# A Fourier-mixing and expert kernel: step A's start, four of its groups, and the order of its first loads are changed

## The chip, the cores and the metric

The kernel runs on one core of a Trainium2 chip. The metric is the device time of one execution in microseconds (us), the median of several runs. Lower is better.

## The reference

The input x is 4 sequences of 3008 rows with 256 channels, float32. Each sequence goes through a real Fourier transform along its rows; the spectrum is multiplied by a complex 256 x 256 matrix, gets a bias, is shrunk towards zero by 0.01 (real and imaginary parts apart) and is transformed back. The 12032 rows then pass a feed-forward block whose weights arrive as 64-bit floats:

```python
X = np.fft.rfft(x, axis=1)
Yr = Xr @ w_r - Xi @ w_i + b_r
Yi = Xr @ w_i + Xi @ w_r + b_i
Yr = np.sign(Yr) * np.maximum(np.abs(Yr) - lam, 0.0)      # Yi alike
y = np.fft.irfft(Y, n=x.shape[1], axis=1)
h = x @ w_in                                              # 256 -> 2048
g = np.maximum(h, 0.0) + alpha * np.minimum(h, 0.0)
return (g @ w_out).astype(np.float32)                     # 2048 -> 256
```

## The kernel before

A transform of length 3008 = 47 x 64 is done in two steps of matrix products. **Step A** (`a_mm`, `a_evac`) multiplies the rows by a table of 94 x 96; a sequence has 16 groups of 512 columns. **Step B** (`b_load`, `b_mm`, `b_evac`, `b_evac2`) is the second half, in 12 blocks q, each on data that a DMA has reordered. **M** (`m_mm`, `m_evac`) mixes channels and shrinks. **C** (`c_mm`, `c_evac`) and **D** (`d_load`, `d_mm`, `d_part`) transform back; between them the data goes through DRAM (`zd`). Then come the two layers of the expert block, `l1_step` and `l2_step` for the first part of the rows and a form with fewer products (`s_l1`, `s_l2`) for the rest. The Fourier stages of sequences 1 to 3 are laid between the expert steps of the sequence before. Sequence 0 has nothing to hide behind, and the change lies there.

A product of float32 operands takes two passes of TensorE here. The other way is to split an operand into a high and a low fp32r part (`split`: ScalarE copies the high part, another engine subtracts it to get the low one) and to make three fp32r products. Step A of sequences 0 and 1 uses float32 and the table `lf_s`; sequences 2 and 3 use `a_split` and the split table `la_s` (L392 to L394). The mixing weights `wr_s`, `wi_s` are split once, in `split_mix`, from tiles that `load_mix` fetches.

The order of work is written out by hand; each engine executes its own instructions in that order. At the start SyncE (SP) issues the loads: eight pairs of groups of x, four slices of the table rb, four groups of sequence 1, the mixing weights, more of rb, two blocks of raw expert weights (`conv_load`). GpSimd (POOL) issues small tables and the bias. TensorE executes products of a zeroed tile `idle` (`keep_warm`) that nothing reads: 36 ahead of step A, 70 ahead of step B, 12 ahead of step D. Step A runs through the 16 groups of sequence 0 and 4 of sequence 1, with three PSUM buffers (tag "f"); even groups are evacuated by ScalarE (ACT), odd ones by VectorE (DVE), those of sequence 1 by ScalarE. After group 15, POOL issues six DMAs (L420) that bring blocks q = 0 to 2 of the evacuated `a0_s` into `bt`, which has three buffers; `split_mix` and `bias_parts` follow. The tiles of two of the later ScalarE evacuations (tags "Yt", "Yc") are those that `bias_parts` reads from.

Then a loop over t = 0 to 12 does `b_mm(t)`, `m_mm(t-1)`, `c_mm(t-3)` on TensorE and, on the other engines, evacuations and `pump(n)`: n portions of the conversion of raw 64-bit expert weights into two fp32r parts, on ScalarE, VectorE and GpSimd. The list `PT` says how many portions belong to each t. In the same loop stand the later loads: `b_load(t+3)`, rb, cf, and rows of sequence 1 (`a_load(1, g)`), among them one group of eight DMAs (g = 6). SP and ScalarE issue DMAs into eight completion semaphores in turn; a DMA waits for the one that had its semaphore before. After the loop, `TAIL` finishes M and C, loads D's first input (`d_load`) and fills the wait with ten groups of step A of sequence 1 (`a_fill`).

Of the kernel before, what the change touches and what calls it, by code (L numbers as in the profile page):

```python
# [93 lines left out]
def fft_mix_moe(ctx, tc, x, w_r, w_i, b_r, b_i, w_in, w_out, alpha, la, rb, lc, rd, lf, cf, sel, out):  # L94
    nc = tc.nc
# [35 lines left out]
    V, G, A, PE = nc.vector, nc.gpsimd, nc.scalar, nc.tensor  # L131

    def f(t):
        return t.bitcast(F32)

    def split(src, hi, lo, e_hi, e_lo):

        if e_hi is A:
            A.activation(out=hi, in_=src, func=AF.Copy)
        else:  # L140
            e_hi.tensor_copy(out=hi, in_=src)
        e_lo.tensor_tensor(out=lo, in0=src, in1=f(hi), op=ALU.subtract)


    la_s = const.tile([NP, 2, NQ], F32R, name="la_s")
# [37 lines left out]
    def first_bias():  # L183

        raw = work.tile([4, 2, C], F32, tag="Yt", name="bias_f", bufs=1)
        hi = work.tile([4, 2, C], F32R, tag="Yc", name="bias_h", bufs=1)
        pick = work.tile([4, 129], F32, tag="ot", name="sel", bufs=1)
        nc.gpsimd.dma_start(out=pick, in_=sel)
        for i, b in enumerate((b_r, b_i)):
            for k in range(2):  # L190
                nc.gpsimd.dma_start(out=raw[2 * i:2 * i + 2, k], in_=b.unsqueeze(0).to_broadcast([2, C]))
        rows = const.tile([128, 2, C], F32R, tag="bias", name="bias_p")
        ones = const.tile([128, 128], F32R, tag="wd", name="ones")
        V.memset(f(rows), 0.0)
        V.memset(f(ones), 0.0)
        bias[0] = ones, rows

        def parts():
            V.memset(lam_s, -LAM)
            V.tensor_copy(out=ones[0:4], in_=pick[:, 0:128])  # L200
            V.tensor_copy(out=hi, in_=raw)
            V.scalar_tensor_tensor(out=rows[0:4], in0=f(hi), scalar=pick[:, 128:129], in1=raw, op0=ALU.mult, op1=ALU.add)

        return parts
# [20 lines left out]

    def split_mix():
        for t, w in zip(mix_w, mix):
            split(t, w[:, 0], w[:, 1], A, G)
        mix_w.clear()

    def combine_mix():
# [22 lines left out]
    def conv_load():  # L254

        m, i = divmod(conv_m[0], 2)
        conv_m[0] += 1
        k = conv_m[0] % 3
        raw = cw_s[:, NSLOT + 8 * k:NSLOT + 8 * k + 8].rearrange("p (k n) f -> p k (n f)", k=2)
        raw = raw.rearrange("p k (n w) -> p k n w", w=2)  # L260
        src = w_out.bitcast(U32)[256 * m:256 * m + 256] if i else w_in.bitcast(U32)[:, 512 * m:512 * m + 512]
        nc.sync.dma_start(out=raw.rearrange("p k n w -> p k (n w)"), in_=src.rearrange("(k p) f -> p k f", p=128))
        conv_raw.append((raw, m, i))
# [70 lines left out]
    def put(*queues):  # L334
        for n, (o, i) in enumerate(stores):
            (queues or (nc.sync,))[n % max(len(queues), 1)].dma_start(out=o, in_=i)
        stores.clear()
# [3 lines left out]
    def a_load(b, g):  # L341

        if g == 0:
            ad[b] = dram.tile([NQ, R, C], F32, tag="ad", name=f"ad{b}")
        src = x[b].rearrange("(p r) c -> p r c", r=R)[:, 4 * g:4 * g + 4]
        if b == 0:
            ts = [x_s[:, 4 * g:4 * g + 4]]
        elif b == 1 and g in X1_TAGS:
            tags = X1_TAGS[g]
            ts = [work.tile([NP, 4 // len(tags), C], F32, tag=tag, name="xt", bufs={"Yl": None, "gh": 4}.get(tag, 1))  # L350
                  for tag in tags]
        else:
            ts = [work.tile([NP, 4, C], F32, tag="xt", name="xt")]
        if (b, g) == (0, 0):
            ts = [ts[0][:, 0:2], ts[0][:, 2:4]]
        n = 4 // len(ts)
        for i, t in enumerate(ts):

            for p in ((0, 80), (80, NP)):
                nc.sync.dma_start(out=t[slice(*p)], in_=src[slice(*p), n * i:n * i + n])  # L360
        xt[b, g] = ts
# [8 lines left out]
    xp = {}  # L370

    def a_split(b, g):

        t, = x_rows(b, g)
        hi = work.tile([NP, 2, C], F32R, tag="xh", name="xh")
        lo = work.tile([NP, 2, C], F32R, tag="xl", name="xl")
        split(t, hi, lo, A, V)
        xp[b, g] = hi, lo
# [3 lines left out]
    def a_mm(b, g):  # L382
        ps = ps_f.tile([NQ, 2, C], F32, tag="f", name="ps_a")
        pa[b, g] = ps
        if b < 2:
            ts = x_rows(b, g)
            n = 2 // len(ts)
            for i, t in enumerate(ts):
                PE.matmul(ps[:, n * i:n * i + n], lf_s, t, start=True, stop=True)
            return  # L390
        hi, lo = xp.pop((b, g))
        PE.matmul(ps, la_s[:, 0], hi, start=True, stop=False)  # L392
        PE.matmul(ps, la_s[:, 1], hi, start=False, stop=False)
        PE.matmul(ps, la_s[:, 0], lo, start=False, stop=True)  # L394

    def a_evac(b, g):
        ps = pa.pop((b, g))
        if b == 0:
            st = a0_s[:, g]
        else:  # L400
            tag = A1_TAGS[g] if b == 1 and g < len(A1_TAGS) else "zst"
            st = work.tile([NQ, 2, C], F32, tag=tag, name="ast", bufs={"bt": 3, "zst": 3, "Yt": 1, "Yc": 1}.get(tag))
        if b == 0 and g % 2:
            V.tensor_copy(out=st, in_=ps)
        else:
            A.activation(out=st, in_=ps, func=AF.Copy)
        if b:
            stores.append((ad[b][:, 2 * g:2 * g + 2], st))
# [562 lines left out]
    PAT = [0, 0] + [1] * 46  # L971
    NG = R // 2
    EARLY = 4
    FILL = 14
    C0 = 2
    PT = [1, 2, 3, 3, 3, 3, 3, 3, 3, 3, 4, 4]
    TAIL = [['me', 1], ['ce', 3], ['cm', 2], ['cm', 1], ['ce', 2], ['ce', 1], ['d'], ['f', 4], ['e'], ['f', 6]]
    WARM = 70
    A1_TAGS = ("zst", "zst", "Yt", "Yc", "bt", "bt", "bt", "Xh", "Xl", "Xh", "Xl", "zst", "zst", "Yc")
    X1_TAGS = {4: ("Yl", "Yl"), 5: ("os", "Yt"), 6: ("gh",) * 4}  # L980
    idle = const.tile([128, 128], BF16, name="idle")

    def keep_warm(n):
        ps = ps_f.tile([128, 512], F32, tag="f", name="ps_idle")
        for _ in range(n):
            PE.matmul(ps[:, 0:128], idle, idle, start=True, stop=True)

    with tc.manual_schedule():
        nc.gpsimd.dma_start(out=lf_s, in_=lf)
        bias_parts = first_bias()  # L990
        nc.gpsimd.dma_start(out=la_s, in_=la)
        V.memset(idle, 0.0)
        keep_warm(36)
        for g in range(NG // 2):
            a_load(0, g)
        load_rb(0, 4)
        for g in range(EARLY // 2):
            a_load(1, g)
        load_mix("Yh", "Yh")
        load_rb(4, 12)  # L1000
        conv_tags.update(v1=("yh", "yl"), ex=("xh", "xh"), lf=("xl", "xl"))
        for _ in range(C0):
            conv_load()
        seq = [(0, g) for g in range(NG)] + [(1, g) for g in range(EARLY)]

        for n, (b, g) in enumerate(seq):
            a_mm(b, g)
            if n >= 1:
                a_evac(*seq[n - 1])
            if n == NG:  # L1010
                for q in range(3):
                    b_load(0, q)
                split_mix()
                bias_parts()
        a_evac(*seq[-1])
        half(0)
        put()
        load_tables()
        keep_warm(WARM)

# [3 lines left out]

        a1 = [EARLY]
        hold = []

        def a_fill(n):
            for g in range(a1[0], min(a1[0] + n, FILL)):
                a_mm(1, g)  # L1030
                a_evac(1, g)
                a1[0] = g + 1

        for t in range(NPAIR + 1):
            run(b_mm, t)
            run(b_load, t + 3)
            run(c_evac, t - 4)
            run(b_evac, t)
            run(m_evac, t - 2)
            run(m_mm, t - 1, ps_h)  # L1040
            run(b_evac2, t)
            run(c_mm, t - 3)
            if t < NPAIR:
                pump(PT[min(t, len(PT) - 1)])
            if t in (2, 5):
                load_rb(2 * t + 8, 2 * t + 14)
            if t < 8 and t % 2 == 0:
                load_cf(3 * t, 3 * t + 6)
            if 5 <= t < 10:
                a_load(1, t - 3)  # L1050
            if t == 10:
                half(1)
                conv_m[1] = FT
# [17 lines left out]
                {"me": m_evac, "cm": c_mm, "ce": c_evac}[op](0, NPAIR - args[0])  # L1071
        V.tensor_scalar(out=beta_s, in0=alpha_s, scalar1=-1.0, scalar2=1.0, op0=ALU.mult, op1=ALU.add)
        conv_tags.update(v1=("xh", "xl"), ex=("Yh", "Yh"), lf=("Yl", "bt"))
        keep_warm(12)
        for c in range(2):
            d_open(c)
            d_step(0, c)
# [22 lines left out]
        for b in range(B):  # L1100
# [9 lines left out]
            if b == 0:  # L1110
                for g in range(FILL, NG):
                    i = 6 * (g - FILL) + 9
                    if g % 2 == 0:
# [84 lines left out]
        for k in range(len(spairs) + SLAG):  # L1198
# [9 lines left out]
            if k >= SLAG:  # L1208
                n, t = spairs[k - SLAG]
# [43 lines left out]
```

## Time and profile before

| | |
|---|---|
| median of 3 runs | 1350.11 us (1349.89 to 1350.86) |
| the profiled execution's own time | 1351.47 us |
| its span in the profile | 1349.7 us |
| TensorE (PE) busy | 1334.4 us, 99% of the span |
| TensorE weight loads (PEld) | 1250.5 us, 93% |
| VectorE (DVE) | 1035.8 us, 77% |
| ScalarE (ACT) | 760.9 us, 56% |
| GpSimd (POOL) | 379.0 us, 28% |

Busy time is the time in which an engine has an instruction at work; matmuls are pipelined, so a busy TensorE is not one at its peak. The span goes from the first to the last instruction; about 1.8 us of the execution lie outside it. The times of rows count from the span's start. A releaser (after "<-") is what ended an engine's idle time, as inferred from semaphores. "SPq" and "ACTq" are DMA issues on the queues of those engines.

### The profile page before, as it was taken

The page shows a single profiled execution, that of the slowest core. Times are in us where ns is not written, and L with a number is a line of the kernel's source. Part 1 is how long each engine was busy: PE and PEld are TensorE (multiplying, and loading weights), DVE is VectorE, ACT ScalarE, POOL GpSimd, SP SyncE. Part 2 cuts the span into 40 slices and gives each one's busy share as a digit, 9 for nine tenths or more (in the row PEclk, how much of TensorE's full clock was granted, in tenths as well). Part 3 has the DMA queues.
Part 4 walks back from the last instruction along what each step waited for, and adds up shares of the span by engine and source line. Part 5 has one row for each costly group of instructions (what it writes and reads, how often), then busy time and mean ns, then how long its engine had stood idle before and what let it go on. Part 6 is the DMA issues. An engine that isn't in the chain of part 4 may idle for free.

```text
span 1349.7 us, 25116 instructions
## 1 busy us (share of the span) xinstructions
PE 1334.4 (99%) x9200; PEld 1250.5 (93%) x9200; DVE 1035.8 (77%) x1934; ACT 760.9 (56%) x1527; POOL 379.0 (28%) x403
## 2 busy tenths in 40 slices
PE   8999999999999999999999999999999999999998
PEld 5979999999999999999999999999999999999998
DVE  2767856776777777776778888888888888888885
ACT  3566655665565555555555555655555556555553
POOL 4854742222221222222121211121112112221222
PEclk9999999999999999999999999999999999999999
DMA  9964223342333312111110110111011101110001
GB/s 244 252 197 136 81 95 105 109 136 72 98 113 114 113 52 79 52 58 41 35 36 2 40 28 5 36 28 28 7 34 28 29 7 34 28 28 9 20 17 28
DMA packets 88117, 89.64 MB, mean 66 GB/s; under 512 B 42317, under 2 KB 70448, under 8 KB 87995
## 3 DMA queue, kind: packets, MB, share of 16 engines
q1 hardware_dynamic: 79700, 77.02, 20.0%
q0 software_dynamic: 5168, 8.02, 2.3%
q10 hardware_dynamic: 3127, 3.01, 0.7%
q8 instruction: 72, 1.18, 0.4%
q14 instruction: 50, 0.41, 0.1%
HBM read 50.49 MB, written 34.34 MB: 63 GB/s over the span
## 4 chain that ended last, share of the span: by engine, by line
PE 90%; DMA 3%; DVE 2%; issue 1%; ACT 1%; SPq 1%; POOL 0%; ACTq 0%; DVEq 0%; POOLq 0%
PE ps_h L791 24%; PE ps_h L686 14%; PE ps_m L488 6%; PE ps_o L893 6%; PE ps_o L894 6%; PE ps_o L892 6%; PE ps_d L617 4%; PE ps_o L725 3%; PE ps_o L724 3%; PE ps_o L723 3%; PE ps_b L428 2%; PE o_last L724 1%; PE o_last L725 1%; PE o_last L723 1%; PE o_last L892 1%; PE o_last L893 1%
## 5 line engine op out<-in xcount | busy, mean ns | idle before, releaser
L791 PE MATMUL ps_h<-yh,w 128*128 128x512 f32 (+1 forms) x960 | 315.6, 390 | 0.0
L830 POOL TENSOR_TENSOR l<-t,h 128x512 fp32r<-128x512 f32 x98 | 127.0, 1296 | 496.5 <-ACT h L828 456.6
L791 PEld LDWEIGHTS ps_h<-yh,w 128*128 128x128 f32 x960 | 180.0, 188 | 33.2
L795 DVE SCALAR_TENSOR_TENSOR sq<-sq,beta_s,ps_h 128x512 f32<-128x512 f32 (+1 forms) x240 | 168.0, 733 | 55.0 <-ACT sq L794 54.2
L686 PE MATMUL ps_h<-yh,w 128*128 128x384 f32 (+1 forms) x704 | 206.8, 336 | 0.9 <-DVE q L693 0.9
L791 PE MATMUL ps_h<-yl,w 128*128 128x512 f32 (+1 forms) x480 | 186.3, 388 | 0.0
L693 DVE SCALAR_TENSOR_TENSOR q<-q,beta_s,ps_h 128x384 f32<-128x384 f32 (+1 forms) x192 | 115.5, 602 | 85.3 <-ACT q L692 83.5
L697 ACT ACTIVATE gh<-q 128x384 fp32r<-128x384 f32 (+1 forms) x192 | 99.1, 516 | 144.5 <-DVE q L693 143.5
L698 POOL TENSOR_TENSOR gl<-q,gh 128x384 fp32r<-128x384 f32 (+1 forms) x90 | 96.6, 1074 | 263.2 <-ACT gh L697 256.4
L810 ACT ACTIVATE dh<-sq 128x768 fp32r<-128x768 f32 x112 | 94.7, 846 | 117.9 <-DVE sq L795 75.2
L794 ACT ACTIVATE sq<-ps_h 128x512 f32<-128x512 f32 (+1 forms) x240 | 133.1, 586 | 27.5 <-PE ps_h L791 23.1
L686 PEld LDWEIGHTS ps_h<-yh,w 128*128 128x128 f32 x704 | 129.4, 189 | 3.8 <-issue 0.8
L828 ACT ACTIVATE h<-t 128x512 fp32r<-128x512 f32 x98 | 62.0, 633 | 105.0 <-DVE t L826 101.7
L686 PE MATMUL ps_h<-yl,w 128*128 128x384 f32 (+1 forms) x352 | 116.5, 331 | 0.0
L692 ACT ACTIVATE q<-ps_h 128x384 f32<-128x384 f32 (+1 forms) x192 | 91.7, 478 | 42.5 <-PE ps_h L686 41.0
L725 PE MATMUL ps_o<-w,gl 128*128 128x256 f32 x384 | 108.0, 281 | 1.7 <-POOL gl L698 1.7
L724 PE MATMUL ps_o<-w,gh 128*128 128x256 f32 x384 | 107.8, 281 | 0.0
L723 PE MATMUL ps_o<-w,gh 128*128 128x256 f32 x384 | 107.7, 281 | 0.0
L791 PEld LDWEIGHTS ps_h<-yl,w 128*128 128x128 f32 x480 | 90.6, 189 | 13.6
L825 DVE TENSOR_TENSOR dl<-sq,dh 128x768 fp32r<-128x768 f32 x98 | 93.5, 954 | 3.8 <-ACT dh L810 3.8
L894 PE MATMUL ps_o<-l,sw_a 128*128 128x256 f32 x294 | 82.0, 279 | 0.0
L892 PE MATMUL ps_o<-h,sw_a 128*128 128x256 f32 x294 | 81.9, 279 | 0.0
(214 smaller groups left out, 3620.2 us busy)
## 6 DMA issues: line engine op xcount, KB each, us to landing
zt<-zd SPq DMA_DIRECT2D x32, 384.0 KB
zd<-zst SPq DMA_DIRECT2D x37, 256.0 KB
ad<-ast SPq DMA_DIRECT2D x48, 192.0 KB
bt<-ad SPq DMA_DIRECT2D x72, 128.0 KB
xt<-in_x SPq DMA_DIRECT2D x21, 320.0 KB
out<-oT SPq DMA_DIRECT2D x152, 32.0 KB
cw_s<-in_moe_w_in SPq DMA_DIRECT2D x8, 512.0 KB
cw_s<-in_moe_w_out SPq DMA_DIRECT2D x8, 512.0 KB
```

The lines of the kernel that those rows point to most:

```text
L686: PE.matmul(ps, wi_h[m // FH][:, w, ct, 128 * (m % FH):128 * (m % FH) + 128], a[:, ct, 0:n], start=(k == 0), stop=(k == 3 * CT - 1))
L693: V.scalar_tensor_tensor(out=q, in0=q, scalar=beta_s[:, m:m + 1], in1=ps, op0=ALU.mult, op1=ALU.add)
L697: A.activation(out=hi, in_=q, func=AF.Copy)
L723: PE.matmul(a, hi[:, t], w[:, 0], start=(i, k) in first, stop=False)
L724: PE.matmul(a, hi[:, t], w[:, 1], start=False, stop=False)
L725: PE.matmul(a, lo[:, t], w[:, 0], start=False, stop=(i, k) in last)
L791: PE.matmul(ps, wi_h[m // FH][:, w, ct, 128 * (m % FH):128 * (m % FH) + 128], a[:, ct, 0:w1], start=(k == 0), stop=(k == 3 * CT - 1))
L794: A.activation(out=q[:, j], in_=ps, func=AF.Relu, scale=-1.0)
L795: V.scalar_tensor_tensor(out=q[:, j], in0=q[:, j], scalar=beta_s[:, m:m + 1], in1=ps, op0=ALU.mult, op1=ALU.add)
L830: G.tensor_tensor(out=l24, in0=t24, in1=f(h24), op=ALU.subtract)
L892: PE.matmul(o, wh, gh, start=first, stop=False)
L894: PE.matmul(o, wh, gl, start=False, stop=last)
```

## The change

Step A's first products of the idle tile are 22 instead of 36, and the tile is zeroed first; the 70 ahead of step B become 24, and the 12 ahead of D go. Groups 9, 11, 13 and 15 of sequence 0 are split into fp32r parts, two groups ahead of their product. The table `la_s` is loaded before the bias. The low parts of the mixing weights are subtracted on VectorE instead of GpSimd. The first two blocks of raw expert weights are loaded after the first store of sequence 1's step A (the order on SP is then store, two loads, other stores). The first portions of the conversion go from t = 0 to t = 2 (the sum stays). Rows of sequence 1 for g = 2 to 6 are loaded at t = 7 to 11 instead of 5 to 9.

```diff
     def split_mix():
         for t, w in zip(mix_w, mix):
-            split(t, w[:, 0], w[:, 1], A, G)
+            split(t, w[:, 0], w[:, 1], A, V)
...
     def a_mm(b, g):
-        if b < 2:
+        if (b, g) not in xp:
...
+    SPLIT = (9, 11, 13, 15)
-    PT = [1, 2, 3, 3, 3, 3, 3, 3, 3, 3, 4, 4]
+    PT = [0, 2, 4, 3, 3, 3, 3, 3, 3, 3, 4, 4]
-    WARM = 70
+    WARM = 24
...
+        V.memset(idle, 0.0)
         nc.gpsimd.dma_start(out=lf_s, in_=lf)
+        nc.gpsimd.dma_start(out=la_s, in_=la)
         bias_parts = first_bias()
-        nc.gpsimd.dma_start(out=la_s, in_=la)
-        V.memset(idle, 0.0)
-        keep_warm(36)
+        keep_warm(22)
...
-        for _ in range(C0):
-            conv_load()
         seq = [(0, g) for g in range(NG)] + [(1, g) for g in range(EARLY)]
         for n, (b, g) in enumerate(seq):
             a_mm(b, g)
             if n >= 1:
                 a_evac(*seq[n - 1])
+            if n + 2 in SPLIT:
+                a_split(0, n + 2)
             if n == NG:
                 for q in range(3):
                     b_load(0, q)
                 split_mix()
                 bias_parts()
+            if n == NG + 1:
+                put()
+                for _ in range(C0):
+                    conv_load()
...
-            if 5 <= t < 10:
-                a_load(1, t - 3)
+            if 7 <= t < 12:
+                a_load(1, t - 5)
...
-        keep_warm(12)
         for c in range(2):
             d_open(c)
             d_step(0, c)
```

## Rows read from the trace of the kernel before

**Rows 1.** The page's chain that ended last, shares of the span by engine.

```profile
PE 90%; DMA 3%; DVE 2%; issue 1%; ACT 1%; SPq 1%; POOL 0%; ACTq 0%; DVEq 0%; POOLq 0%
```

**Rows 2.** TensorE in order of time, 0 to 31.4 us: start, duration, instructions.

```profile
1.68 3.62 PE L986 MATMUL ps_idle<-idle 128*128 128x128 bf16 x36 [1.68 <-DVE idle L992]
5.13 14.28 PE L389 MATMUL ps_a<-x,lf_s 94*96 94x512 f32 x32
...
23.00 1.10 PE L389 MATMUL ps_a<-xt,lf_s 94*96 94x512 f32 x2 [1.00 <-ACT ast L406]
23.94 4.07 PE L986 MATMUL ps_idle<-idle 128*128 128x128 bf16 x70
28.57 1.76 PE L428 MATMUL ps_b<-rb_s,bt 128*128 128x128 f32 x12 [0.55 <-issue]
```

**Rows 3.** POOL in order of time: its DMA issues of bt.

```profile
20.80 4.10 POOL L420 DMA_DIRECT2D bt<-a  x6 [15.73 <-DVE bias_h L201]
```

**Rows 4.** bt: issue to landing, windows 20.7:21.5, 45.4:47, 52:53.6.

```profile
DMA to landing us min/median/max: 7.7/7.7/7.7
...
DMA to landing us min/median/max: 4.4/4.6/4.8
...
DMA to landing us min/median/max: 9.8/10.6/11.4
```

**Rows 5.** Stretches: length, busy PE, PEld, DVE, ACT, POOL, clock, DMA share, GB/s.

```profile
20.80:24.30 3.50, 2.50 (x12) 0.94 (x12) 0.58 (x1) 2.87 (x6) 3.50 (x6) 1.00 1.03 395
24.30:28.50 4.20, 3.71 (x67) 3.54 (x64) 0.00 (x0) 0.43 (x1) 3.10 (x3) 1.00 1.08 230
```

**Rows 6.** TensorE in order of time, four pieces between 62 and 102 us.

```profile
64.28 0.71 PE L428 MATMUL ps_b<-rb_s,bt 128*128 128x128 f32 x4 [0.74 <-DMA bt<-a]
...
84.71 0.50 PE L468 MATMUL ps_m<-bias_p,ones 128*128 128x512 f32 x1 [0.82 <-DVE Y L502]
...
91.95 8.76 PE L389 MATMUL ps_a<-xt,lf_s 94*96 94x512 f32 x24
100.54 0.84 PE L986 MATMUL ps_idle<-idle 128*128 128x128 bf16 x12
```

**Rows 7.** The chain in order of time, to 17 us: start, duration, what.

```profile
9.69 6.48 DMA x<-in_x
...
16.18 5.64 DMA wm_f<-in_w_i
```

**Rows 8.** ScalarE in order of time: the last evacuation of sequence 0.

```profile
18.59 0.59 ACT L406 ACTIVATE a<-ps_a 96x512 f32<-96x512 f32 x1 [1.12 <-PE ps_a L389]
```

**Rows 9.** VectorE in order of time: its last evacuation, and the end of bias_parts.

```profile
19.45 0.69 DVE L404 COPY a<-ps_a 96x512 f32<-96x512 f32 x1 [1.03 <-PE ps_a L389]
...
20.64 0.74 DVE L202 SCALAR_TENSOR_TENSOR bias_p<-bias_h,sel,bias_f 4x512 fp32r<-4x512 f32 x1
```

**Rows 10.** Lines L139, L142: splits of sequences 2, 3: ns min/median/max, first and last.

```profile
L139 ACT ACTIVATE xh<-xt x32: 614/618/625, 228.6 to 456.3; 94x512 fp32r<-94x512 f32 x32
...
L142 DVE TENSOR_TENSOR xl<-xt,xh x32: 680/689/690, 230.3 to 457.0; 94x512 fp32r<-94x512 f32 x32
```

**Rows 11.** TensorE in order of time: two of three fp32r products of a later group.

```profile
235.41 0.40 PE L393 MATMUL ps_a<-xh,la_s 94*96 94x512 f32 x1
235.65 0.39 PE L394 MATMUL ps_a<-xl,la_s 94*96 94x512 f32 x1
```

**Rows 12.** Stretches of L986 alone: length, PE, PEld, clock, DMA share, GB/s.

```profile
1.60:4.70 3.10, 3.02 (x29) 3.02 (x30) 1.00 0.75 212
4.70:5.30 0.60, 0.59 (x10) 0.42 (x7) 1.00 0.95 251
```

**Rows 13.** The chain in order of time, 60 to 80 us.

```profile
60.01 11.21 DMA xt<-in_x
...
71.23 5.67 DMA xt<-in_x
```

**Rows 14.** ScalarE in order of time, about 77 us.

```profile
77.45 0.60 ACT L442 ACTIVATE Xh<-ps_b 128x512 fp32r<-128x512 f32 x1 [3.03 <-DMA xt<-in_x]
```

## The prediction

> **What bounds the kernel now.** I read the page's chain of the work that ended last first. The reader sees that TensorE carries 90% of it [rows 1], and DMA, VectorE and the other engines 1 to 3% each. So the expert stages, which fill most of the span, are TensorE working without a pause, and nothing in this change touches their products. What the change touches is the beginning, where the chain is not TensorE's. For that I read TensorE in order of time [rows 2]. Step A of sequence 0 starts at 5.13 us, right behind 36 idle products; its 16 groups take two passes each and 0.86 us a group. The four groups of sequence 1 end at 23.94 with the last one held up to 23.00 by a ScalarE evacuation. Then come 70 idle products up to 27.95, a pause of 0.55 us for which no engine is named, and step B at 28.57. The idle products are not the reason for that start. POOL's issues tell it [rows 3, 4]: the first DMA of bt is issued at 20.80 and needs 7.7 us to land, so it lands at 28.5, when step B starts. The fastest bt loads of the same size, later, need 4.4 to 4.8 us [rows 4]. Between issue and landing the DMA engines are full, at 395 and then 230 GB/s [rows 5]: among the traffic are 1.05 MB of raw expert weights that are not needed for several steps. So the start of step B is set by a DMA that shares the engines with less urgent ones. From there to 92 us TensorE is almost without gaps; the two that I count are 0.74 us for a bt landing and 0.82 us for VectorE [rows 6]. After 91.95 the fill and 12 idle products lead to step D, without a pause.
>
> **Step A's start.** With the idle tile zeroed first, TensorE can start at about 1.1 instead of 1.68, and 22 products instead of 36 end some 1.7 us sooner. I give this nothing. The loads of x set the pace: the last pair of groups is issued at 9.69 and lands at 16.17 [rows 7]. The first product of group 14 stood at 17.5 (5.13 plus 14.28, less the last product's 0.59 and three steps of 0.43). So at most 1.3 us can be had at the end of step A, whatever starts sooner.
>
> **The four split groups.** On TensorE three fp32r products at 0.24 us each [rows 11] take 0.72 instead of 0.86: four times 0.14 is 0.6 us. But each split adds 0.62 us to ScalarE and 0.69 to VectorE [rows 10], between evacuations of 0.59 and 0.69 [rows 8, 9] that come every 1.72 us on each. That would fit, were it not for the order. The low part of group 9 stands on VectorE ahead of the evacuation of group 7, and waits for its high part, which stands on ScalarE behind the evacuation of group 6. Counted back from the last evacuations in steps of 1.72: group 6 is evacuated at 11.71 to 12.30, the high part ends at 12.92, the low part at 13.61, and the evacuation of group 7 at 14.30 instead of 13.26. Group 10 takes over that PSUM buffer and starts at 14.35 instead of 14.1. Repeated for 11, 13 and 15 with the same durations, the last evacuation of sequence 0 ends at 20.5 instead of 20.14. So I cost step A at +0.4; bounds are -1.5 (only x limits: 16.17, then 0.86, 0.72, 0.17 to drain and 0.69 to evacuate, 18.6) and +1.8 (the clock, below).
>
> **Step B's start.** Two things must be there. TensorE must be free: the mixing weights land at 21.82 [rows 7], which the change doesn't move (nothing ahead of them in SP's queue changes). ScalarE splits them (0.62) and evacuates the first group of sequence 1 (0.59), to 23.0; the group that waited ends at 23.94 as before; 24 idle products at 0.058 (4.07 over 70) end at 25.35. The low parts of the weights, now on VectorE behind ScalarE's high parts, end at about 23.2. `bias_parts` follows them there and takes 1.25 (19.45 plus 0.69 to 20.64 plus 0.74 [rows 9]): 24.5. The two last evacuations of step A wait for it, since they reuse its tiles, and end at 25.2 and 25.8. Step B's first PSUM buffer is free at 25.2, so this added wait is just covered by the idle products. POOL loses two subtractions, but it stood idle behind them.
> The other is bt. It is issued between 20.55 and 21.15; the lag of 0.66 behind the last evacuation may or may not stay. I take 20.9. The two raw weight blocks now follow the store of 23.0, so bt goes first. I take the 4.6 us of the window about 46 us [rows 4] rather than 7.7, because the engines have less queued up at 21 us now. The first half lands at 25.5, the second 0.7 later, and step B starts as if at 25.65: **-2.9 us**. Bounds: -3.2 (TensorE's 25.35) and 0 (7.7 us again).
>
> **The loop over t.** TensorE fills it, so its end moves with its start. Rows of sequence 1 (0.75 MB at t = 5 and 6) no longer compete with the bt that came 0.74 late, and the load that held ScalarE for 3.03 [rows 13, 14], behind which TensorE later waits 0.82, comes at another place. Together 1.56; I take -1.1, because the 1.05 MB of weights come in later. Bounds are -1.6 and +2.0, the latter if a bt load of 11.4 us [rows 4] comes at a step that now has 2.9 us less. Raw weights that come late hold ScalarE at t = 1; a wait of 3.03 there cost TensorE 0.82 once, and I take none of it.
>
> **Step D.** Twelve idle products at 0.058 go: **-0.7**. What hides behind them is the load of D's input; if it lands later than the fill ends, this term is 0.
>
> **Sum.** -2.9, -1.1 and -0.7 (step A's +0.4 is in the first) are -4.7 us. The profiled execution took 1351.47, its span 1349.7 and 1.8 around it; that gives 1346.8 there. It was 1.36 above the median of 1350.11, on whose scale it is **1345.4**.
>
> **Rivals.**
> *The transfers take it back.* The DMA engines are at 1.03 to 1.08 already [rows 5], and 1.05 MB at 230 GB/s are 4.6 us of their time, moved behind step B's start. If each bt load then lands as late on the clock as before, TensorE waits for it in the loop and keeps only the 0.7 and perhaps part of the 1.1: 1348.3 to 1349.4. For it: the full engines, and bt loads of 9.8 to 11.4 us. Against it: the rows of sequence 1 leave the same stretch, about as many bytes.
> *The clock.* The trace shows that 29 idle products take 3.10 us up to 4.70 and 10 take 0.60 after it [rows 12]: 0.107 and 0.06 each, the levels of 1.2 and 2.4 GHz, with the rise 3.0 us after TensorE's first product. In the new order the idle products begin at about 1.1 and 22 of them end at 3.4; step A's first data need not be there by then (by 5.13 they were [rows 2]), and the third group waits for its own load as before, so TensorE may pause twice. If the rise then comes only after 3.0 us of unbroken work that begin with the third group, at about 7 (5.13 and two groups of 0.86), step A runs at half speed to 10: three us at half speed are 1.5 us of work, 1.8 with the pauses, and -1.1 is left at step B, -2.9 in all, 1347.2. The Trainium skill, "TensorE: Matmul & The Clock Gate", Part 1, says that the array begins throttled and that only sustained activity lifts it, which speaks against a shorter warm-up. By that rule the sum would be this one; the trace agrees as far as the rise after 3.0 us of unbroken products goes, and no row shows a broken run.
> *Slower: the stores behind the eight row loads.* The eight DMAs of g = 6 now stand at t = 11, and the last stores of step C take their completion semaphores after them, on ScalarE, which waits in order. A row load once took 5.67 us and once 11.21 to land [rows 13], and held ScalarE for 3.03 [rows 14]. In the loop later steps absorbed most of that. At the end nothing does: store, load of D's input and D follow one another, and the fill is evacuated by the same ScalarE. Issued about 82 to 86 on the old clock, the rows land at 88 to 97, the stores stand at 86 to 92; a hold of 7 us gives -4.7 + 7 = +2.3, 1352.4. It decides from a hold of 4.7 us on, that is a landing of some 9 us; against it, most of the other loads are done by then.
>
> **Chances and range.** Forecast (1344 to 1347.4) 0.62; transfers 0.19; clock 0.09; slower 0.08, the rest somewhere between. What a measurement of this kernel can tell from no change is about 0.2%, 2.7 us. Faster by more has the forecast and most of the clock: 0.70. Within it are the transfers and the rest: 0.23. Slower by more: 0.07. The range takes all unknown terms at their good bounds, somewhat short (-6.2), and most of the transfers' case: 1343.9 to 1349.2.
>
> **What would show it.** Step B's first product at 25.3 to 26.2, not 28.57; bt landing 4.4 to 5 us after an issue at 20.6 to 21.2; the evacuation of group 15 ending near 20.5, with VectorE idle until the high part ahead of each low part; the wait at the ninth block's bt gone; no ScalarE wait over 1 us for rows between t = 8 and the end of C; the fill starting near 88 and D directly behind it. The prediction is wrong if bt takes over 6 us, if the loop from step B to the fill is longer than the 63.4 us of before, or if idle products at 0.107 are followed by step A products at half speed beyond 8 us.

## The result: 10 us slower, and the profile after

The changed kernel takes 1360.73 us (median of 8 runs, 1360.26 to 1375.26) against 1350.54 (8 runs, 1349.61 to 1353.0) for the kernel before on the same chip: a ratio of 1.0087 [1.0059, 1.0115]. The forecast was 1345.4 and faster. One of the eight runs took 1375.26 with a mean clock of 0.988, the others 1360.26 to 1361.13 with 0.999 to 1.0; no trace of it was kept and its cause is open. The profiled execution of after took 1361.05 us with a span of 1359.3, 9.6 more than before.

TensorE of after in order of time (start, duration, instructions; in brackets the idle time ahead and its releaser); the lines answer to [rows 2, 6]:

```profile
0.99 2.53 PE L987 MATMUL ps_idle<-idle 128*128 128x128 bf16 x22 [0.99 <-DVE idle L990]
4.52 15.68 PE L389 MATMUL ps_a<-x,lf_s 94*96 94x512 f32 x18 [1.00 <-DMA lf_s<-tab_lf]
...
30.23 7.03 PE L389 MATMUL ps_a<-xt,lf_s 94*96 94x512 f32 x8
37.06 2.77 PE L987 MATMUL ps_idle<-idle 128*128 128x128 bf16 x24
39.62 2.21 PE L428 MATMUL ps_b<-rb_s,bt 128*128 128x128 f32 x16
...
94.33 0.50 PE L468 MATMUL ps_m<-bias_p,ones 128*128 128x512 f32 x1 [0.44 <-DVE Y L502]
99.80 1.13 PE L550 MATMUL ps_c<-Y,cw_s 128*128 128x256 f32 x4 [0.99 <-DVE Y L502]
...
102.28 8.76 PE L389 MATMUL ps_a<-xt,lf_s 94*96 94x512 f32 x24
110.87 2.82 PE L617 MATMUL ps_d<-rd_s,zt 96*128 96x94 f32 x24
```

Step A does start sooner, at 4.52 instead of 5.13. But its first 18 passes take 15.68 us, 0.87 each, where 32 took 14.28 before, 0.45 each. Step B starts at 39.62 instead of 28.57: +11.05. From there to the fill 62.66 us go by (before 63.38: -0.72), from the fill to D 8.59 (before 9.27: -0.68). The sum is +9.65, and the span is 9.6 longer. All of the loss lies ahead of step B.

The durations of single passes say what the loss is. Before, then after (ns, min/median/max, first and last start):

```profile
L389 PE MATMUL ps_a<-x,lf_s x32: 592/592/641, 5.1 to 18.8; 94*96 94x512 f32 x32
```

```profile
L389 PE MATMUL ps_a<-x,lf_s x24: 1055/1061/1170, 4.5 to 28.1; 94*96 94x512 f32 x24
```

The second run of idle products in after, L987 alone (start and end, length, PE, PEld, clock, DMA share, GB/s):

```profile
37.06:39.62 2.56, 2.56 (x24) 2.50 (x23) 1.00 0.94 220
```

24 products in 2.56 us are 0.107 each, the pace of 1.2 GHz as in [rows 12]. So TensorE was at half speed from its first product until about 40 us, through all of step A. The clock column says 1.00 here as it does for the slow products in [rows 12]: in the stretch ahead of a kernel's first rise it can't be used, and the level is read from the products' pace.

The landing of bt took as long as costed. POOL of after, and its first bt issue to landing (us):

```profile
31.82 4.11 POOL L420 DMA_DIRECT2D bt<-a  x6 [26.78 <-DVE a L404]
```

```profile
bt<-a POOLq DMA_DIRECT2D x1, 128.0 KB, 4.6
```

4.6 us, not the 7.7 of [rows 4]. But the issue is at 31.82, not at 20.9, so TensorE, busy with step A to 37, did not wait for it.

### The profile page after: what moved, and what is told of

It is laid out like the page before. It is cut to its first block, busy times and chain, and to the rows that moved or that the text cites. A ratio compares the mean times of both kernels' runs of the same rounds, so it can differ in the third digit from the quotient of the medians.

```text
span 1359.3 us, 24994 instructions
## 1 busy us (share of the span) xinstructions
PE 1346.1 (99%) x9132; PEld 1253.6 (92%) x9132; DVE 1039.1 (76%) x1940; ACT 763.0 (56%) x1531; POOL 376.4 (28%) x401
## 4 chain that ended last, share of the span: by engine, by line
PE 90%; DVE 3%; issue 2%; DMA 2%; ACT 1%; POOL 0%; SPq 0%; ACTq 0%; DVEq 0%; POOLq 0%
PE ps_h L791 24%; PE ps_h L686 13%; PE ps_m L488 6%; PE ps_o L893 6%; PE ps_o L894 6%; PE ps_o L892 6%; PE ps_d L617 4%; PE ps_o L725 3%; PE ps_o L724 3%; PE ps_o L723 3%; PE ps_a L389 3%; PE ps_b L428 2%; PE o_last L724 1%; PE o_last L725 1%; PE o_last L723 1%
```

## The experiments

Each ratio is to the kernel before, run on the same chip. Two theories stood at the start: the clock (22 idle products end before it rises, and step A does not raise it), and the work itself (splits, order of evacuations, late loads).

### Is it the idle products ahead of step A?

The changed kernel with 36 of them:

```diff
-        keep_warm(22)
+        keep_warm(36)
```

> The changed kernel with 36 instead of 22 idle products ahead of step A, nothing else. Clock theory (22 products at 0.107 us end before TensorE's clock rises, and step A's float32 passes never raise it): the pitch of the idle products falls to 0.06 about 3.0 us after the first one, step A's passes take 0.43 us instead of 0.85, step B starts at 25.3 to 26.5 us instead of 39.6, and the time is 1344.5 to 1348. Rival (the four split groups, or transfers, hold step A up whatever the clock does): step A still ends after 30 us and the time stays within 2 us of 1360.7.

Measured: 1353.81 us (11 runs) against 1352.26, ratio 1.001 [1.0, 1.0019]. TensorE:

```profile
1.00 4.02 PE L987 MATMUL ps_idle<-idle 128*128 128x128 bf16 x36 [1.00 <-DVE idle L990]
5.34 1.96 PE L389 MATMUL ps_a<-x,lf_s 94*96 94x512 f32 x4 [0.32 <-DMA lf_s<-tab_lf]
...
24.55 1.50 PE L987 MATMUL ps_idle<-idle 128*128 128x128 bf16 x24
25.89 1.50 PE L428 MATMUL ps_b<-rb_s,bt 128*128 128x128 f32 x8
29.29 2.20 PE L428 MATMUL ps_b<-rb_s,bt 128*128 128x128 f32 x8 [1.90 <-DMA bt<-a]
```

Fourteen more idle products bring back step A at full speed (0.43 to 0.49 a pass), and step B starts at 25.89 where the prediction had 25.65. The ratio falls from 1.0087 to 1.001: the 10 us are the clock. But the forecast does not come with it, nor the 1344.5 to 1348 expected here; that is taken up below.

The kernel before with 22 idle products and nothing else changed:

```diff
-        keep_warm(36)
+        keep_warm(22)
```

> The kernel before with 22 instead of 36 idle products ahead of step A, nothing else. Clock theory: step A at half speed, its 40 passes end near 38.5 us, the clock rises about 3 us into the 70 idle products that follow, step B starts at 43 to 45 us instead of 28.6, and the time is 1361 to 1366, more than the changed kernel's 1360.7. Rival (the shorter warm-up alone is harmless, it is the split groups that do it): within 2 us of 1350.5.

Measured: 1364.48 us (12 runs), ratio 1.0063 [1.0035, 1.0092]. The runs fall in two groups, eight at 1363.9 to 1367.6 and four at 1350.8 to 1355.0. The profiled one is one of the eight:

```profile
1.68 2.53 PE L986 MATMUL ps_idle<-idle 128*128 128x128 bf16 x22 [1.68 <-DVE idle L992]
4.58 27.62 PE L389 MATMUL ps_a<-x,lf_s 94*96 94x512 f32 x32 [0.38 <-DMA lf_s<-tab_lf]
32.00 7.03 PE L389 MATMUL ps_a<-xt,lf_s 94*96 94x512 f32 x8
38.82 4.76 PE L986 MATMUL ps_idle<-idle 128*128 128x128 bf16 x70
```

One number, 22 for 36, makes the whole loss: 27.62 us for the 32 passes that took 14.28. Step A runs here for 34 us without a pause and the clock stays down; in the 70 idle products behind it comes up. They take 4.76 us, against 4.07 at full speed: about 14 of them came at the slow pace, so the rise lay some 1.4 us behind the first and not the 3 that were expected.

36 idle products put into step A behind its fourth group, in the changed kernel:

```diff
             a_mm(b, g)
+            if n == 3:
+                keep_warm(36)
```

> The changed kernel (22 idle products first) with 36 more idle products behind group 3 of step A. Clock theory: groups 0 to 3 at half speed to about 11.4 us, the clock rises 3.0 us into the second run of idle products at about 14.4, the later groups take 0.86 us, step B starts at 30 to 32 us and the time is 1349.5 to 1353. Rival (once the clock has missed its rise it stays low until something other than idle products comes): step A at half speed to its end, 1361 to 1366.

Measured: 1358.2 us (5 runs), ratio 1.0039 [1.0021, 1.0057].

```profile
4.55 7.14 PE L389 MATMUL ps_a<-x,lf_s 94*96 94x512 f32 x8 [1.02 <-DMA lf_s<-tab_lf]
11.48 2.97 PE L987 MATMUL ps_idle<-idle 128*128 128x128 bf16 x36
14.29 4.48 PE L389 MATMUL ps_a<-x,lf_s 94*96 94x512 f32 x10
```

Eight passes take 7.14 us ahead of the idle products, ten take 4.48 behind them. So the clock rose in these (by their spacing 1.7 us behind the first, not 3.0), and what ran before them had not raised it. Step B starts at 31.11, as expected, but the time is above the expected 1349.5 to 1353 and in the trace 5.1 us over before. Groups 0 to 3 at half speed and the idle products are 2.5 us of that, step B's later start. Most of the rest is a second loss of clock: behind waits of 1.29, 1.07 and 1.64 us for bt it fell to half from 33.6 to 40.5 us, which costs up to 3.4. A stretch of it (columns as in [rows 5]):

```profile
36.00:40.00 4.00, 4.00 (x19) 3.90 (x19) 1.02 (x2) 1.18 (x2) 3.10 (x6) 0.50 1.08 312
```

### Are the splits part of it?

The changed kernel without split groups:

```diff
-    SPLIT = (9, 11, 13, 15)
+    SPLIT = ()
```

> The changed kernel (22 idle products) with no group of step A split. Clock theory: step A's 40 passes at 0.85 us end at about 38.7 us instead of 38.1, time 1360.5 to 1362.5. Rival (the order of the splits on VectorE holds step A up): step A ends before 30 us and the time is below 1353.

Measured: 1363.33 us (4 runs), ratio 1.0082 [1.0065, 1.0098].

```profile
4.33 27.62 PE L389 MATMUL ps_a<-x,lf_s 94*96 94x512 f32 x32 [0.81 <-DMA lf_s<-tab_lf]
31.74 7.03 PE L389 MATMUL ps_a<-xt,lf_s 94*96 94x512 f32 x8
38.56 2.74 PE L987 MATMUL ps_idle<-idle 128*128 128x128 bf16 x24
```

The loss is there without them, and the ratios cannot be told apart. At half speed the splits even shorten step A, from 38.56 to 37.06.

### With the clock cured, where is the forecast gain?

In the run with 36 idle products step B starts 2.68 us sooner than before, but D at 102.98 instead of 101.22. From step B to the fill it takes 68.49 us, 5.1 more. Its waits in that stretch sum to 5.4 us against 2.9 before, mostly the 1.90 for bt above. And ScalarE was held by a store out of the tile it wanted to write, which SP had issued behind the raw weights:

```profile
39.36 0.69 ACT L501 ACTIVATE Yc<-ps_m,lam_s 128x512 f32<-128x512 f32 x1 [2.48 <-DMA ad<-ast]
```

So the raw weights behind all four stores:

```diff
-            if n == NG + 1:
-                put()
-                for _ in range(C0):
-                    conv_load()
         a_evac(*seq[-1])
         half(0)
         put()
+        for _ in range(C0):
+            conv_load()
```

> The changed kernel with 36 idle products ahead of step A, and the two raw weight blocks loaded after all four stores of sequence 1's step A instead of after the first. Theory (with the clock cured, the raw weights ahead of three stores and beside the second bt are what takes step B's earlier start back: TensorE waits 1.9 us for bt, its clock falls for 3.4 us, and the first M evacuation waits for the store that frees its tile): bt for q = 1 lands before 28 us, the clock stays up, M's first evacuation comes before 34 us, the fill starts at 89 to 91 us and the time is 2.5 to 5 us below the kernel before. Rival (the engines are full and any order of the same bytes gives the same loop): the fill starts at 93 to 95 us and the time is within 1.5 us of the kernel before.

Measured: 1355.79 us (8 runs), ratio 1.0021 [1.0009, 1.0032]: not faster. The same without split groups:

> As f1, with no group of step A split. Theory (a split stands on VectorE ahead of an older evacuation and costs step A 0.4 to 1.0 us): the last evacuation of sequence 0 ends 0.4 to 1.0 us sooner than with the splits, step B starts as much sooner or is held by its idle products, and the time is 0 to 1 us below f1. Rival (the splits save TensorE 0.6 us): 0.3 to 0.8 us above f1.

Measured: 1354.94 us (12 runs), ratio 1.0019 [1.0008, 1.0031]. The store was not what counted, and the splits make no difference that can be measured here. In both ScalarE waits for the raw weights themselves (6.27 us in the first, 7.03 in the second). In the first TensorE also waits longer for bt than without this edit (1.90); in the second, whose step B starts at 27.68, it does not wait for bt, and the loop to the fill still takes 66.24 us. Of the first:

```profile
38.97 0.66 ACT L275 ACTIVATE conv<-cw_s 128x512 f32<-128x512 f32 x1 [6.27 <-DMA cw_s<-in_moe_w_in]
```

```profile
26.85 0.71 PE L428 MATMUL ps_b<-rb_s,bt 128*128 128x128 f32 x4 [0.29 <-DMA bt<-a]
28.41 0.68 PE L428 MATMUL ps_b<-rb_s,bt 128*128 128x128 f32 x4 [0.84 <-DMA bt<-a]
31.35 0.71 PE L428 MATMUL ps_b<-rb_s,bt 128*128 128x128 f32 x4 [2.26 <-DMA bt<-a]
```

The other way, the raw weights back in their old place, splits and 36 idle products kept:

```diff
+        for _ in range(C0):
+            conv_load()
         seq = [(0, g) for g in range(NG)] + [(1, g) for g in range(EARLY)]
...
-            if n == NG + 1:
-                put()
-                for _ in range(C0):
-                    conv_load()
```

> The changed kernel with 36 idle products and the two raw weight blocks loaded ahead of step A's loop, as in the kernel before. Theory: the first bt lands at 28.5 to 29.5 us again, TensorE idles from 25.9 on since only 24 idle products are left, its clock may fall there, the fill starts at 91.5 to 94 us, and the time is within 1.5 us of the kernel before: the load's place was worth the 2.7 us at step B, and what follows it took that away. Rival (the deferral itself is what costs): 2 us or more below the kernel before.

Measured: 1351.29 us (11 runs) against 1351.75, ratio 0.9997 [0.9988, 1.0005].

```profile
29.30 2.03 PE L428 MATMUL ps_b<-rb_s,bt 128*128 128x128 f32 x16 [3.13 <-issue]
...
91.61 8.76 PE L389 MATMUL ps_a<-xt,lf_s 94*96 94x512 f32 x24
```

bt now lands late again and step B starts at 29.30, 3.4 us later than with late weights; and the kernel is 2.5 us faster than with them (medians 1353.81 to 1351.29; by the ratios 1.7). From step B to the fill it takes 62.31 us instead of 68.49. The late order takes back the early start, and more. Of these 6.2 us 3.4 are TensorE's waits (5.4 us in sum against 2.0) and up to 1.7 a fall of its clock, taken up in the next section; the remaining 1.1 are not placed.

This run also keeps the parts of the change that none tests alone: the earlier `la_s`, the low parts of the mixing weights on VectorE, the portions moved to t = 2. With the splits, the later rows and no idle products ahead of D they make no difference that can be told from none.

The kernel before with only the two edits further on, the rows of sequence 1 later and no idle products ahead of D:

```diff
-            if 5 <= t < 10:
-                a_load(1, t - 3)
+            if 7 <= t < 12:
+                a_load(1, t - 5)
...
-        keep_warm(12)
```

> The kernel before with two parts of the change alone: no idle products ahead of step D, and rows of sequence 1 two steps later in the loop. By the changed kernel's trace these give 0.7 us each (the loop 62.7 instead of 63.4 us, fill to D 8.6 instead of 9.3), so 1.0 to 1.8 us below the kernel before. Rival (the loop is shorter there only because step B started 11 us later, when more had landed): 0.7 us below.

Measured: 1350.85 us (11 runs) against 1351.75, ratio 0.9992 [0.9983, 1.0]. From the fill to D the trace has 8.60 us, 0.67 less, and the waits of [rows 6] are 0 and 0.59. From step B to the fill it has 62.13, 1.25 less, but step B starts at 30.27 in this profile, so later loads had more time here too, and the rival is not ruled out. The gain of 1 us is at the edge of what these runs can tell.

### The second, shorter run of idle products

With 24 products ahead of step B TensorE often stands still until bt lands. The clock in 28.20 to 32.00 of the run with 36 idle products and late weights (length, busy PE, PEld, DVE, ACT, POOL, clock, DMA share, GB/s):

```profile
28.20:32.00 3.80, 2.71 (x11) 2.57 (x12) 0.55 (x1) 0.47 (x1) 2.40 (x6) 0.62 1.04 225
```

It had been up since step A; behind the wait of 1.90 it fell to half from 29.1 to 32.5, then came back. To see whether the pause does it, two kernels with 24 and then the same with more. First without splits and with early weights (the kernel of the 1351.29 us with `SPLIT = ()`):

> The changed kernel with 36 idle products ahead of step A, the raw weights back in their old place and no split groups; what is left of the change is the zeroed tile first, 24 idle products ahead of step B, VectorE's low parts of the mixing weights, the rows of sequence 1 at t = 7 to 11 and no idle products ahead of D. If the splits cost what the prediction put on them (step A's last evacuation 0.4 us later), the issue of bt comes at about 20.9 instead of 21.47 and the whole is 0.4 to 0.6 us under the same kernel with splits: about 1350.8, 0.9 under before. If the splits are free, it is as with them: no difference from before. If bt's landing does not depend on the issue but on the engines' load, step B still starts at 29.0 to 29.5 and the gain is only the one behind step B, about 1.1 us.

Measured: 1352.34 us (11 runs) against 1351.43, ratio 1.0001 [0.9992, 1.001]: no difference from before, as with the splits. Its profile has the fall too, from 31.6 to 35.0, behind waits of 3.03 and 1.15 us. Second, one raw block early and one behind the first store:

```diff
-        for _ in range(C0):
-            conv_load()
+        conv_load()
...
+            if n == NG + 1:
+                put()
+                conv_load()
```

> The same, with the second block of raw weights behind the first store of sequence 1 and the first in the old place. If the raw weights' bytes set bt's landing, half of them gone brings bt from 29.2 to about 27.3, and if the cost of coming late (the next bt load, the stores behind them) is in proportion too, the total is half way between the late and the early order, 1.2 us over the kernel with both early. If only the queue behind the second block counts, it is as bad as with both late, 2.5 us over. If a middle place has the best of both, it is 1 to 2 us under before.

Measured: 1350.67 us (11 runs) against 1351.43, ratio 0.9992 [0.9983, 1.0001]. Step B starts at 28.17, with the clock in its first microseconds:

```profile
28.20:32.00 3.80, 3.80 (x21) 3.63 (x22) 1.09 (x2) 1.62 (x3) 2.28 (x5) 0.66 0.99 249
```

Then the first of them with 70 idle products ahead of step B:

```diff
-    WARM = 24
+    WARM = 70
```

> The kernel with 36 idle products ahead of step A, raw weights in the old place and no split groups, with 70 instead of 24 idle products ahead of step B, so that TensorE has no pause there. If the pauses of 2 to 3 us that the 24 leave are what let the clock fall for 3.4 us behind step B's start (seen in three of the profiles with them and not in that of before), no fall follows, the time is 1.5 to 1.7 us under the same kernel with 24 in the runs that had one: about 1350.3, and 0.8 to 1.2 us under before. If the falls have nothing to do with the pauses, about half of the runs keep them, and the time stays at that of before.

Measured: 1350.92 us (11 runs) against 1352.61, ratio 0.9991 [0.9982, 1.0]. And the second with 64:

```diff
-    WARM = 24
+    WARM = 64
```

> The kernel with one raw weight block in the old place and one behind the first store, no split groups, with 64 instead of 24 idle products ahead of step B (they end at about 28.2, when bt lands). If the pause sets the clock's fall, no fall follows and the time is 1 to 1.7 us under the same kernel with 24, about 1349.2, 2 us under before: a version faster than both. If not, it stays at 1350.7.

Measured: 1350.75 us (11 runs) against 1352.61, ratio 0.9986 [0.9977, 0.9995], the one version of twelve whose interval lies below 1. Its TensorE, and a stretch of it:

```profile
24.62 3.74 PE L987 MATMUL ps_idle<-idle 128*128 128x128 bf16 x64
28.19 1.11 PE L428 MATMUL ps_b<-rb_s,bt 128*128 128x128 f32 x8
29.88 0.68 PE L428 MATMUL ps_b<-rb_s,bt 128*128 128x128 f32 x4 [0.58 <-DMA bt<-a]
31.43 0.71 PE L428 MATMUL ps_b<-rb_s,bt 128*128 128x128 f32 x4 [0.87 <-DMA bt<-a]
...
91.50 8.76 PE L389 MATMUL ps_a<-xt,lf_s 94*96 94x512 f32 x24
100.10 2.81 PE L617 MATMUL ps_d<-rd_s,zt 96*128 96x94 f32 x24
```

```profile
28.20:32.00 3.80, 2.35 (x20) 2.00 (x18) 0.69 (x1) 0.60 (x1) 2.28 (x5) 1.00 1.02 268
```

No fall: 1.00 where the same kernel with 24 had 0.66. By the ratios the gain from more idle products is 0.0010 and 0.0006, 1.4 and 0.8 us, near the 1.5 and the 1 that were expected, but the intervals overlap. The mean clock listed with each run (from its first rise on) says the same: with 24 products and early weights it is 0.997 to 0.999 in 11 runs, median 0.997; with 70 it is 0.998 to 1.0, median 0.999. A pause does not always bring a fall: the run with splits and early weights waited 3.13 us and had a clock of 1.00 over the same stretch. Nor does a fall need a long one at step B: in the run with late weights behind all stores and no splits step B waited 0.38 us, and the clock was at half from 48.4 to 51.8, with waits of 0.79 and 0.66 us ahead of it:

```profile
48.00:52.00 4.00, 4.00 (x20) 3.90 (x20) 3.90 (x6) 2.97 (x5) 3.58 (x6) 0.57 0.86 274
```

Of the seven profiles with 24 products ahead of step B in which step A reached full speed, six have such a fall; of the four with 64 or 70, none. So the longer run keeps the clock up in these profiles; that it is the pause which brings the falls is borne out, not shown.

## Why the prediction was wrong, step by step

**The step that failed** is "Step A's start", costed at nothing because "the loads of x set the pace". It took the clock as given once TensorE is at work; in after all of step A ran at half speed, and step B started 11.05 us later. Nor did the loads of x set the pace in before: 32 passes at 0.43 us and 0.16 to drain are 13.9 of its 14.28 us [rows 2], TensorE's own pace. The rival "The clock" named the place and the cause, 22 idle products that end before the rise, with a pause behind them (1.00 us, for `lf_s`). But it was priced wrong: the rise was to come "after 3.0 us of unbroken work that begin with the third group", whatever work that is, and to cost 1.8 us. In step A of after no rise came in 32.5 us. The rival should have been bounded by the whole of step A at half speed (40 passes at 0.43 more, 17 us, less the waits for x and for evacuations that slower passes hide), and at 9% it was also held too unlikely. [Rows 12] could have warned: the rise came inside the idle products, so no row of before showed that step A can bring it. The page cited there, the Trainium skill's "TensorE: Matmul & The Clock Gate", Part 1, says that the default state is throttled and that activity releases it; this trace agrees with the first, and with the second only behind idle products: step A's float32 passes were sustained and released nothing in 32.5 us.

**Step B's start** (-2.9) was right as a mechanism: in after bt landed 4.6 us behind its issue. With the clock cured the size came out too, -2.68, but partly by luck. bt was issued at 21.79, not 20.9, and took 3.6 us, not 4.6; step B at 25.89 followed the idle products, without a wait for bt:

```profile
21.79 4.11 POOL L420 DMA_DIRECT2D bt<-a  x6 [16.74 <-DVE a L404]
...
bt<-a POOLq DMA_DIRECT2D x1, 128.0 KB, 3.6
```

It was not worth what it said, because the rival "The transfers take it back" was true too. It was held off with the rows of sequence 1 that "leave the same stretch, about as many bytes". They did leave it, but the second block's bt, not the later ones, paid: 1.90 us, and 2.26 in the run with splits and the weights after all stores. The prediction gave the landing of one bt and assumed the other two. The trace of before had the warning in a row that the prediction does not count, a wait for the second block's bt:

```profile
31.00 0.71 PE L428 MATMUL ps_b<-rb_s,bt 128*128 128x128 f32 x4 [0.67 <-DMA bt<-a]
```

Between step B and the fill TensorE waited five times in before, 2.9 us in sum, not the two times (1.56) that the prediction counted. (Its 70 idle products end at 28.0, 23.94 plus 4.07, not 27.95; nothing hangs on that.)

**The loop over t** (-1.1) measured -0.72 in after, and -1.25 in the kernel before with later rows and no idle products ahead of D. Its two waits of 0.74 and 0.82 became 0 and 0.44; a new 0.99 stands at 99.80 for VectorE's part of Y (0.28 in that place before), shortly behind a ScalarE evacuation that the row loads, now later, had held:

```profile
98.34 0.69 ACT L501 ACTIVATE Yc<-ps_m,lam_s 128x512 f32<-128x512 f32 x1 [1.14 <-DMA xt<-in_x]
```

**Step D** (-0.7) measured -0.68, and -0.67 in the kernel with that edit and the rows alone. D's input was there.

**The four split groups** (+0.4): the order acted as described, the size was too high. In the run with 36 idle products VectorE stood idle for ScalarE's high part ahead of each low part, 1.31 us for group 9 and 0.43 to 0.50 for the others:

```profile
13.82 0.69 DVE L142 TENSOR_TENSOR xl<-x,xh 94x512 fp32r<-94x512 f32 x1 [1.31 <-ACT xh L139]
```

From group 8's first product to sequence 1's first it took 7.05 us there (13.34 to 20.39), against 6.87 in before (12.38 to 19.25): +0.18. The total times cannot tell this from nothing (1.0087 and 1.0082, 1.0021 and 1.0019, 0.9997 and 1.0001, with and without splits).

**The slower rival**, stores behind the eight row loads, shows in the trace of after at most as this hold of 1.14 us; it needed 4.7 to decide.

What stays open: whether fewer idle products or the 1 us pause behind them keeps the clock down (after had both). For the count speaks that the kernel before with 22 had a pause of only 0.38 in its profile and stayed down, by their times in eight of twelve runs, while the changed kernel with 36, on the same chip, paused for 0.32 and came up. Open too: why step A does not raise the clock. In the run with 36 and late weights, of the 5.1 us lost behind step B's start 2.5 are waits and up to 1.7 the clock; 0.9 I cannot place.

## What to carry to other kernels

Before idle products are cut, find the row from which their spacing halves (0.107 to 0.058 us here), in more than one profile, since it moves by microseconds. Do not count on the real work behind them to bring that about unless a row shows it doing so: the price of a missed rise is then the whole stage at half speed, not the microseconds saved. An idle run that fills a wait for a DMA is cheap cover; shorten it only together with the wait. And when one transfer is moved ahead of others, follow the next transfer of the same kind, not only the first.

## What the runs showed of the chip that was not expected

Float32 products of 94x96 with 512 columns, without a pause for 34 us, left TensorE at 1.2 GHz; with bf16 products of a zeroed tile that nothing reads it came to 2.4, within the 70 of the kernel before with 22, and in after at the first products of step B behind its 24. Once at 2.4 GHz, the same float32 products ran on at 0.43 us a pass to the end of step A. In the ten profiles with 36 idle products ahead of step A the rise lay 3.0 to 5.3 us behind the first of them, and in six it came only after the last, at most 1.5 us after. The prediction's 3.0 was one draw of this. In the longest cases the rise lies a little into step A. The kernel with early weights, no splits and 70 products shows it by its longest pass (ns, min/median/max):

```profile
L389 PE MATMUL ps_a<-x,lf_s x32: 592/592/1114, 4.8 to 20.3; 94*96 94x512 f32 x32
```

So it is not shown that step A's products can't be at work when the clock rises, only that they did not raise it alone. The outcome of 22 idle products differs from run to run of one kernel by 13 us. The same page of the Trainium skill, Part 1, says that the number of slow products varies from run to run; the two groups of runs agree, but here the variation decides over a whole stage and not over a few products.
